# One chunk of a row's contraction moved ahead, a wider selection and a split product in the tail of an adaLN decode block

## The chip, the cores and the metric

The kernel runs on one core of a Trainium2 chip. The metric is the device time of one execution in microseconds, as the median over runs. All matmuls are fp32; the profile shows each fp32 matmul as two instructions (two passes) on TensorE, which is called PE in the profile (its weight loads: PEld). VectorE is DVE, ScalarE is ACT, GpSimd is POOL, SyncE is SP.

## What is computed

A decode step for four batch rows, one token each, D = 512, with a modulation from a conditioning vector c:

```python
mod = (silu(c) @ w_mod).reshape(4, 6, 1, -1)
sa, ca, ga, sb, cb, gb = (mod[:, i] for i in range(6))
h = layernorm(x) * (1 + ca) + sa
x = x + ga * attention(h, k_cache, v_cache, wq, wo)   # 32 query heads, 8 kv heads, 4096 positions, 128 wide
h = layernorm(x) * (1 + cb) + sb
u = gelu(einsum("bsd,sf->bdf", layernorm(h), w1) + b1)  # S = 1, F = 1792
y = einsum("bdf,fs->bds", u, w2) + b2
x = x + gb * transpose(y)
```

As there is one token per row, the mixer's first product is an outer product of the 512 channels with 1792 hidden units, followed by gelu and a weighted sum over the hidden units.

## The kernel before, in words

The 4 x 8 pairs of batch row and kv head are numbered 0 to 31. For each of them one 2 MB key tile and one 2 MB value tile come from memory on the SP queue. The steps for a pair are scores (line 216), the maximum over rows and columns (lines 224 to 247), the exponential on ACT (249), 32x32 transposes on DVE (253), the product with the values (275 to 293), a copy (301), a selection that folds the four column groups of the result into one vector per head (`pick`, 308), a scaling by the sum (321), the projection with wo (326) and the sum over heads (342).

Batch row b's mixer starts when its eight pairs are done. The hidden units are cut into 14 chunks of 128 (NF = 14). DVE expands a chunk (line 423), ACT applies the gelu, PE contracts the chunk with w2. For rows 0 to 2 a chunk's contraction is one matmul of 512 columns into one of four column groups of 32, chosen by the chunk's number (`contract_wide`, 433); the four groups are folded at the end (`gather_up`, 495). For the last row, row 3, each chunk is four matmuls of 128 columns, one for each column group (`contract`, 427), in `finish` (527).

Pairs 0 to 23 run in a loop. From pair 24 on, the order is written out by hand in the string PLAN (625 to 634): each word is one step, and the words' order is the order in which every engine's queue gets its instructions. Small letters and capitals are different steps; "s26" is the scores of pair 26, "a27" the selection of pair 27, "p31" the projection of pair 31. "x" expands two chunks of row 2, "g" applies the gelu to the oldest expanded pair of chunks, "c" contracts the oldest pair that has had its gelu. "f" scales one block of wo with the gate. The loads are the words with L. The engines run through their queues in order and wait for each other by semaphores.

The last line of PLAN is the tail, behind the last projection p31: "zs" takes the statistics of row 3 on DVE (line 363); "zq" starts the sums over all partitions with a small matmul that adds the epsilon (line 372); "zg" adds the statistics to it by a second matmul (line 377), which waits for zs; "c" twice contracts the chunks 10 to 13 of row 2, the chunks 12 and 13 lying in a spare piece of a load buffer, which the profile names kv; "zx" copies the row; "zm" normalises and modulates it into h (lines 394 to 404); "zq" and "zg" do the second statistics; "zb0" and "zb1" spread h over the partitions (line 411); "zw0" makes the first of the four parts (k = 0 to 3) of the last modulation product, the gate gb (`modmm`, 196); "zn" normalises; "zc" folds row 2's contraction (line 353). T2 and T3 make ACT load the tables of the square root and the gelu. Then `finish` runs row 3's 14 chunks in seven groups, makes the rest of the gate's product behind chunk 1 (line 540), and writes the output.

Selection. The result of the product with the values has four column groups; `pick` folds them with a matmul whose moving operand has four columns, one per query head. WIDE (line 24) repeats these columns for some pairs: for pair 27 (NS - 5) the four columns are repeated 24 times, so 96 columns move, and for pair 28 32 times, so 128 columns. Only the first four columns of the result are read:

```python
WIDE = {NS - 5: 24, NS - 4: 32}
...
n, m = po.shape[-1] // DH, WIDE.get(i, 1)
pt = ps_m.tile([P, m, REP], F32, name="pt", tag="m")
OT[i] = pt[:, 0]
```

Of the kernel before, what the change touches and what calls it, by code (L numbers as in the profile page):

```python
# [19 lines left out]
NS = B * HKV  # L20
NSM = 3 * NF + 16 + 1


WIDE = {NS - 5: 24, NS - 4: 32}
NARROW = NS - 3


# [1 line left out]
def adaln_decode(ctx: ExitStack, tc: tile.TileContext, small, x, wmod, wq, kk, kv, vv, wo, out):  # L29
# [166 lines left out]
    def modmm(pm, t, ks=range(4)):  # L196
        for k in ks:
            for c in range(4):
                mm(pm[32 * c:32 * c + 32, :], sT8[:, k].rearrange("p b r -> p (b r)"),
                   WM[t][:, k, c * P:(c + 1) * P], start=(k == 0), stop=(k == 3))  # L200
# [107 lines left out]
    def pick(i):  # L308
        po = PV.pop(i)
        n, m = po.shape[-1] // DH, WIDE.get(i, 1)  # L310
        if i in OT:
# [38 lines left out]
    def fold_groups(pool, acc, tag):  # L350
        pc = pool.tile([P, P], F32, name="pc", tag=tag)
        for c in range(4):
            mm(pc[32 * c:32 * c + 32, :], first, acc[:, c * P:(c + 1) * P], start=True, stop=True)
        return pc
# [68 lines left out]
    def expand(u, hb, wr, js):  # L423
        for e, j in enumerate(js):
            dv.tensor_scalar(u[:, e, :], hb, wr[:, j:j + 1], b1[:, j:j + 1], op0=OP.mult, op1=OP.add)  # L425

    def contract(py, u, js):
        for e, j in enumerate(js):
            for c in range(4):
                mm(py[32 * c:32 * c + 32, :], w2[:, j:j + 1].to_broadcast([P, 32]),  # L430
                   u[:, e, c * P:(c + 1) * P], start=(j == 0), stop=(j == NF - 1))

    def contract_wide(py, u, js):
        for e, j in enumerate(js):
            q = j % 4
            mm(py[32 * q:32 * q + 32, :], w2[:, j:j + 1].to_broadcast([P, 32]), u[:, e, :],  # L436
               start=(j < 4), stop=(j >= NF - 4))

    class Mixer:
# [48 lines left out]
        def consume(self, most=9):  # L488
# [3 lines left out]
                (contract_wide if self.wide else contract)(self.py, u, js)  # L492
            del self.done[:most]

        def gather_up(self):
            yw = wk.tile([P, D], F32, name="yw", tag="yw", bufs=1)
            dv.tensor_copy(yw, self.py)
            self.py = fold_groups(ps_e, yw, "e")
# [27 lines left out]

    def finish(b, pg, py, hb, wr):
        uu = ring.tile([P, 16, D], F32, name="uu", tag="kv")
        for js in ((0,), (1,), (2, 3, 4), (5, 6, 7), (8, 9, 10), (11, 12), (13,)):
            j = js[0]  # L530
            if j < 2:
                nc.scalar.activation(uu[:, j], hb, AF.Gelu_apprx_tanh, bias=b1[:, j:j + 1], scale=wr[:, j:j + 1])
                u = uu[:, j:j + 1]
            else:
                u = uu[:, j:j + len(js)]
                expand(u, hb, wr, js)
                nc.scalar.activation(u, u, AF.Gelu_apprx_tanh)  # L537
            contract(py, u, js)
            if j == 1:
                modmm(pg, 5, (1, 2, 3))  # L540
        mix.close()
        dv.tensor_mul(osb[:, :B - 1], ZK, pg.unsqueeze(1).to_broadcast([P, B - 1, P]))
        dv.tensor_add(osb[:, :B - 1], osb[:, :B - 1], XK[:, :B - 1])
        gbl = cst.tile([P, P], F32, name="gbl")
        dv.tensor_copy(gbl, pg)
        dst = out.rearrange("b (c n) -> b c n", c=4)
        for e in range(B - 1):
            (nc.scalar if e == B - 2 else nc.sync).dma_start(dst[e], osb[8 * e:P:32, e])
        dv.scalar_tensor_tensor(osb[:, b], py, b2, gbl, op0=OP.add, op1=OP.mult)
        dv.tensor_add(osb[:, b], osb[:, b], XK[:, b])  # L550
        nc.sync.dma_start(dst[b], osb[8 * b:P:32, b])
# [23 lines left out]
    mix = None  # L575
    for i in range(NS - HKV):
# [22 lines left out]
        if i and i % HKV == 0:  # L599
            mix = Mixer(i // HKV - 1)  # L600
# [14 lines left out]
        if i == NS - HKV - 2:  # L615
# [4 lines left out]
    mix, row = Mixer(B - 2), Mixer(B - 1)  # L620
# [9 lines left out]
    LV28 L28 a27 g X30 t29.1 t29.0 l29 L29 s31 A27 LV29 b30 p27 x B30 S31 c c m31 e30 P27 X31 v28.0 f LT LV30  # L630
    b31 v28.1 B31 f e31 LV31 l30 V28 L30 t30.1 l31 L31 a28 t31.1 A28 p28 v29.0 v29.1 t30.0 f P28 V29 v30.0 a29
    v30.1 A29 LW p29 f v30.2 v30.3 t31.0 P29 g V30 Y y a30 A30 p30 E x v31.0 f v31.1 v31.2 v31.3 V31 z31 a31 I A31 p31
    zs g zq zg T2 c zx c zm zq zb0 T3 zg zb1 zw0 zn zc
    """
    TABLE = {"s": scores, "S": row_max, "m": turn_max, "X": col_max, "b": spread_max, "B": copy_max, "e": expo,
             "l": sums, "L": scale, "V": copy_v, "a": pick, "A": copy_o, "P": add_up,
             "LP": load_pair}
    MIX = {"F": mix.fold, "R": mix.residual, "G": mix.gather, "M": mix.modulate, "H": mix.gather, "Q": mix.spread,
           "N": mix.normalise, "g": mix.gelu, "c": lambda: mix.consume(1), "zc": mix.gather_up, "zq": row.gather_eps,
           "zg": row.gather,  # L640
           "zm": row.modulate, "zn": row.normalise}
    for step in PLAN.split():
        op, k = step.rstrip("0123456789."), step.lstrip("abcdefghijklmnopqrstuvwxyzABCDEFGHIJKLMNOPQRSTUVWXYZ")
# [52 lines left out]
        elif op == "zb":  # L696
            if i == 0:
                py = ps_s.tile([P, 8, P], F32, name="py3", tag="s")
            row.spread(py[:, 4:], (2 * i, 2 * i + 1))
    finish(B - 1, pgx[:, 0], py[:, 0], row.hb, row.wr)  # L700


# [32 lines left out]
```

## Time and profile before

| | us |
|---|---|
| median of 3 runs | 387.23 (387.15 to 387.37) |
| the profiled execution's own time | 387.3 |
| its span, first to last instruction | 385.2 |
| PE busy | 295.1 (77% of the span) |
| DVE busy | 195.4 (51%) |
| ACT busy | 111.5 (29%) |
| memory read | 157.32 MB, 408 GB/s over the span |
| share of the last chain in transfers | 54% |
| mean granted PE clock | 0.892 |

All lines come from one execution, whose time line starts with the first instruction. A line of the time line has the start in us, the time that the merged group takes in us, engine, line of the kernel, operation, destination and sources, shapes and count; in brackets stands the idle time of the engine just before and what ended it. In the chain of waits, each piece of time is put down to the instruction which the end was waiting for just then. In a table by stretches, each engine's busy time is followed by the number of its instructions, and PEclk is the granted clock of TensorE as a share of full speed.

### The profile page before, as it was taken

The page shows a single profiled execution, that of the slowest core. Times are in us where ns is not written, and L with a number is a line of the kernel's source. Part 1 is how long each engine was busy: PE and PEld are TensorE (multiplying, and loading weights), DVE is VectorE, ACT ScalarE, POOL GpSimd, SP SyncE. Part 2 cuts the span into 40 slices and gives each one's busy share as a digit, 9 for nine tenths or more (in the row PEclk, how much of TensorE's full clock was granted, in tenths as well). Part 3 has the DMA queues.
Part 4 walks back from the last instruction along what each step waited for, and adds up shares of the span by engine and source line. Part 5 has one row for each costly group of instructions (what it writes and reads, how often), then busy time and mean ns, then how long its engine had stood idle before and what let it go on. Part 6 is the DMA issues. An engine that isn't in the chain of part 4 may idle for free.

```text
span 385.2 us, 5574 instructions
## 1 busy us (share of the span) xinstructions
PE 295.1 (77%) x2376; PEld 116.2 (30%) x2376; DVE 195.4 (51%) x386; ACT 111.5 (29%) x141; POOL 8.5 (2%) x30
## 2 busy tenths in 40 slices
PE   0865778865856939879877868799777897999984
PEld 0111122311223303334322322343222353344653
DVE  0120252620442614664766545648665566788756
ACT  1001111121110111112567211115674103758166
POOL 1200000000000000000000000000000000000000
PEclk9998555985995886998999998989999998999999
DMA  8999999999999999999999999999999999999920
GB/s 331 436 436 436 407 456 436 407 439 429 423 444 432 424 436 432 434 436 434 436 435 436 434 433 430 425 429 427 432 434 432 430 432 424 432 423 427 416 101 3
DMA packets 7408, 157.68 MB, mean 409 GB/s; under 512 B 964, under 2 KB 1236, under 8 KB 1496
## 3 DMA queue, kind: packets, MB, share of 16 engines
q1 hardware_dynamic: 7376, 157.33, 95.2%
q8 instruction: 18, 0.29, 0.3%
q14 instruction: 6, 0.05, 0.0%
q10 hardware_dynamic: 8, 0.00, 0.0%
HBM read 157.32 MB, written 0.01 MB: 408 GB/s over the span
## 4 chain that ended last, share of the span: by engine, by line
DMA 54%; PE 32%; DVE 8%; ACT 4%; issue 1%; POOL 1%; SPq 0%; ACTq 0%
DMA kv<-in_kv 42%; PE s L221 10%; PE pv L281 7%; DMA wm<-in_wmod 5%; DMA kv<-in_kk 4%; DVE m L226 3%; PE s L113 2%; DVE p L257 2%; DMA sm<-in_small 2%; PE pa L332 2%; PE pt L318 1%; PE pb L241 1%; ACT uu L537 1%; PE pm L205 1%; PE pve L293 1%; PE pm L230 1%
## 5 line engine op out<-in xcount | busy, mean ns | idle before, releaser
L221 PE MATMUL s<-kv,QT 128*32 128x512 f32 x512 | 79.0, 745 | 42.1 <-DMA kv<-in_kv 38.5
L226 DVE TENSOR_REDUCE m<-s 128x1 f32<-128x1024 f32 x32 | 39.2, 1224 | 101.9 <-PE s L221 101.7
L251 ACT ACTIVATE p<-s,nm 128x1024 f32<-128x1024 f32 x32 | 35.6, 1114 | 182.7 <-DVE nm L246 182.6
L281 PE MATMUL pv<-kv,p 128*32 128x512 f32 x464 | 67.1, 646 | 0.5 <-DMA kv<-in_kv 0.5
L221 PEld LDWEIGHTS s<-kv,QT 128*32 128x32 f32 x512 | 16.5, 126 | 88.5 <-DMA kv<-in_kv 54.8
L318 PEld LDWEIGHTS pt<-g,po 128*128 128x128 f32 x236 | 30.4, 200 | 28.5 <-issue 21.2
L332 PE MATMUL pa<-wo,oT 128*32 128x512 f32 x240 | 33.6, 633 | 4.6 <-DVE oT L324 4.5
L318 PE MATMUL pt<-g,po 128*128 128x4 f32 (+2 forms) x236 | 33.1, 264 | 1.5 <-DVE po L304 1.0
L257 DVE STREAM_TRANSPOSE p<-p 128x1024 f32<-128x1024 f32 x25 | 30.8, 1233 | 0.0
L304 DVE COPY po<-pv 128x512 f32<-128x512 f32 x29 | 20.0, 688 | 15.5 <-PE pv L281 15.5
L235 DVE TENSOR_REDUCE mx<-pm 1x128 f32<-1x512 f32 x32 | 21.3, 669 | 1.1 <-PE pm L230 1.1
L425 DVE TENSOR_SCALAR u<-hb,wr,sm 128x512 f32<-128x512 f32 x40 | 19.9, 539 | 1.9 <-POOL wr L420 1.0
L481 ACT ACTIVATE u<-u 128x1024 f32<-128x1024 f32 x20 | 20.4, 1051 | 1.5 <-DVE u L425 1.4
L251 ACT ACT_TABLE_LOAD x11 | 14.1, 1283 | 20.4 <-DVE nm L246 20.4
L348 DVE TENSOR_TENSOR acc<-acc,pa 128x512 f32<-128x512 f32 x26 | 17.8, 686 | 3.1 <-PE pa L332 3.1
L241 PEld LDWEIGHTS pb<-neg,mx 1*128 1x128 f32 x64 | 10.0, 194 | 26.9 <-DVE mx L235 25.2
L113 PE MATMUL s<-wm,sT 128*4 128x512 f32 x16 | 9.0, 725 | 11.3 <-DVE sT L99 11.3
L481 ACT ACT_TABLE_LOAD x13 | 16.7, 1283 | 0.2
L281 PEld LDWEIGHTS pv<-kv,p 128*32 128x32 f32 x464 | 13.3, 146 | 6.2 <-issue 2.3
L230 PE MATMUL pm<-ident,m 128*1 128x128 f32 x32 | 9.2, 286 | 7.6 <-DVE m L226 3.5
L241 PE MATMUL pb<-neg,mx 1*128 1x1 f32 x64 | 12.7, 265 | 2.1 <-DVE mx L235 2.1
L436 PE MATMUL py<-u,sm 128*32 128x512 f32 x80 | 13.5, 593 | 0.4 <-ACT u L481 0.4
(134 smaller groups left out, 207.9 us busy)
## 6 DMA issues: line engine op xcount, KB each, us to landing
kv<-in_kv SPq DMA_DIRECT2D x28, 4096.0 KB, 21.9
wq<-in_wq SPq DMA_DIRECT2D x2, 4096.0 KB, 16.2
wo<-in_wo SPq DMA_DIRECT2D x4, 2048.0 KB
kv<-in_kv SPq DMA_DIRECT2D x4, 2048.0 KB, 19.5
wm<-in_wmod SPq DMA_DIRECT2D x2, 2048.0 KB, 14.4
kv<-in_kk SPq DMA_DIRECT2D x1, 4096.0 KB
kv<-in_vv SPq DMA_DIRECT2D x3, 1024.0 KB
wm<-in_wmod SPq DMA_DIRECT2D x1, 1024.0 KB
```

The source lines that it names most:

```text
L221: mm(s[32 * c:32 * c + 32, n * 512:(n + 1) * 512], QT[:, b, h, :], KT[i][:, (n * 4 + c) * 512:(n * 4 + c + 1) * 512], start=True, stop=True)
L226: dv.tensor_reduce(M[i], S[i], axis=AX.X, op=OP.max)
L235: dv.tensor_reduce(mx, M[i].rearrange("o (c r) -> o r c", c=4).unsqueeze(1).to_broadcast([1, 4, 32, 4]), axis=AX.X, op=OP.max)
L241: mm(pb, M[i].rearrange("o c r -> o (c r)"), neg1, start=True, stop=True)
L251: nc.scalar.activation(p, S[i], AF.Exp, bias=M.pop(i), accum_out=l)
L257: dv.transpose(PL[i][0], PL[i][0])
L281: mm(PV[i][32 * q:32 * q + 32, :], pT[:, 128 * k:128 * k + 128:4], VT[i][:, 4 * k:4 * k + 4, :].rearrange("p j d -> p (j d)"), start=(k < ...
L304: dv.tensor_copy(PV[i], pv)
L318: mm(pt, po[:, c * DH:(c + 1) * DH], sel.unsqueeze(1).to_broadcast([P, m, REP]), start=(c == 0), stop=(c == n - 1))
L332: mm(pa[32 * g:32 * g + 32, :], oT[:, g:g + 1].to_broadcast([P, 32]), wo_t[h][:, g, :], start=True, stop=True)
L425: dv.tensor_scalar(u[:, e, :], hb, wr[:, j:j + 1], b1[:, j:j + 1], op0=OP.mult, op1=OP.add)
L481: nc.scalar.activation(u, u, AF.Gelu_apprx_tanh)
```

## The change

There are three edits.

1. Pair 27's selection moves 128 columns (32 repeats) instead of 96 (24 repeats).
2. A new step "k" (`consume_one`) contracts one chunk, the first of the oldest pair of chunks that has had its gelu, and leaves the other one in the list. It stands behind the first "zq" and ahead of "zg" in the tail's line of PLAN. The first of the two "c" steps then contracts one chunk in place of two.
3. In `finish`, part k = 1 of the last modulation product goes ahead of chunk 0; parts 2 and 3 stay behind chunk 1.

```diff
-WIDE = {NS - 5: 24, NS - 4: 32}
+WIDE = {NS - 5: 32, NS - 4: 32}
...
+        def consume_one(self):
+            u, js = self.done[0]
+            contract_wide(self.py, u, js[:1])
+            self.done[0] = (u[:, 1:], js[1:])
...
     def finish(b, pg, py, hb, wr):
         uu = ring.tile([P, 16, D], F32, name="uu", tag="kv")
+        modmm(pg, 5, (1,))
         for js in ((0,), (1,), (2, 3, 4), (5, 6, 7), (8, 9, 10), (11, 12), (13,)):
...
             if j == 1:
-                modmm(pg, 5, (1, 2, 3))
+                modmm(pg, 5, (2, 3))
...
-    zs g zq zg T2 c zx c zm zq zb0 T3 zg zb1 zw0 zn zc
+    zs g zq k zg T2 c zx c zm zq zb0 T3 zg zb1 zw0 zn zc
...
-           "N": mix.normalise, "g": mix.gelu, "c": lambda: mix.consume(1), "zc": mix.gather_up, "zq": row.gather_eps,
+           "N": mix.normalise, "g": mix.gelu, "c": lambda: mix.consume(1), "k": mix.consume_one, "zc": mix.gather_up, "zq": row.gather_eps,
```

## The prediction

> **What bounds the kernel now.** I read three views: the slices of the page (where the transfers end), the chain of waits from there on, and the TensorE (PE) instructions in order of time around each edit. In the page's 40 slices (9.6 us each, busy share in tenths) the transfers read:
>
> ```profile
> DMA  8999999999999999999999999999999999999920
> ```
>
> The reader is to see that the 16 DMA engines are at 8 or 9 to the end of slice 38, 366 us, at 2 in the next and at 0 in the last. Until about 367 us (the last wait for a load, quoted below, ends at 367.14) the transfers set the time; after it comes a tail of 18 us in which no load is awaited. No edit touches a load. So only what lies on the chain of the tail can count; here is its middle and its end.
>
> ```profile
> 370.40 0.40 PE pst L377 x2
> 370.81 0.99 PE py L436 x8
> 371.80 0.33 PE pst L372 x2
> 372.13 0.03 issue
> 372.16 0.68 PE py L411 x4
> ...
> 375.87 4.11 ACT uu L537 x3
> 379.99 0.01 issue
> 379.99 1.05 ACT uu L537
> 381.04 0.04 issue
> 381.09 0.99 PE py L430 x24
> ```
>
> The statistics of row 3 go DVE (stm), PE (pst, line 377), DVE again, and come back to PE as the spread of h (py, line 411). From there ScalarE's gelus run without a hole to 381.04, and the last contraction and the output follow. The last chain is serial: what is lost at line 377 is lost at the end. Around it PE does this:
>
> ```profile
> 369.70 0.40 PE L372 MATMUL pst<-epsr,ones 1*128 1x24 f32 x2
> 370.40 0.40 PE L377 MATMUL pst<-stm,ones 128*128 128x24 f32 x2 [0.31 <-DVE stm L367]
> 370.74 0.62 PE L436 MATMUL py<-u,sm 128*32 128x512 f32 x2
> 370.75 0.62 PE L436 MATMUL py<-kv,sm 128*32 128x512 f32 x2
> 371.19 0.60 PE L436 MATMUL py<-u,sm 128*32 128x512 f32 x2
> 371.20 0.60 PE L436 MATMUL py<-kv,sm 128*32 128x512 f32 x2
> 371.73 0.40 PE L372 MATMUL pst<-epsr,ones 1*128 1x24 f32 x2
> ...
> 373.48 0.42 PE L199 MATMUL pgx<-kv,sT 128*32 128x128 f32 x8
> ```
>
> Each fp32 matmul is two instructions (passes). The four chunks of the two steps "c" (10 and 11 from u, 12 and 13 from kv) go to four column groups: all four first passes start at 370.74 to 370.75, all four second ones at 371.19 to 371.20. They run side by side.
>
> **The change, part by part.** *The chunk moved forward (step k).* It issues one matmul, two passes of 512 columns, and two weight loads, on PE alone; no transfer, no other queue. Chunk 10 had its gelu long before (the pair's gelu is the step "g" behind P29), so k waits for nothing. It is put between line 372 at 369.70 and line 377 at 370.40, where PE stands idle for 0.31 us. What it takes there, from the rows: a pair of small matmuls followed by a 512-column pass is 370.74 - 370.40 = 0.34 apart, so k starts at 369.70 + 0.34 = 370.04. Its second pass uses the same column group and comes 371.19 - 370.74 = 0.45 later, 370.49. From a last 512-column pass to the next matmul over all columns is 371.73 - 371.20 = 0.53, so line 377 starts at 371.02 instead of 370.40: 0.62 us late. Queued behind k is just this matmul, and DVE waits for it (mean and variance), then h, then all of the tail.
>
> What k takes away later: the block at 370.74 has three chunks instead of four, and as they run side by side it is no shorter; gain 0. Could PE make good the delay before the spread at line 411? That needs h, which comes through DVE from line 377:
>
> ```profile
> 371.66 0.35 DVE L403 SCALAR_TENSOR_TENSOR h<-a,ye,prep 128x128 f32<-128x128 f32 x1
> ```
>
> h is done at 372.01, PE is done with line 372 at 372.13, and the spread starts at 372.16: the two paths meet within 0.12 us, and both hang on line 377. So the delay passes whole. Bounds: at the least, no drain at either border, a start 0.24 behind 369.70 (the closest distance between the pair at 348.26 and the scores at 348.50 below) and two passes of 0.45 end at 370.84, 0.44 late; at the most the whole block of 0.99 from the chain is set behind line 372's end at 370.10, 371.09, 0.69 late. I take 0.62, since its three distances are from neighbours of the same shapes.
>
> The Trainium skill, page "TensorEngine Tiling (Array Packing)", section "Key Properties", says that changing the tiling mode drains TensorE. The trace agrees as far as it goes: 0.53 from pass to full-width matmul against 0.45 from pass to pass. Without that rule the sum would be 0.44 late, with it 0.62; k adds one such change each way.
>
> *Head 27 in 32 columns instead of 24.* Four matmuls, eight passes, move 128 columns instead of 96; only the first four of the result are read. Head 28 already has that shape, so its price stands in the trace:
>
> ```profile
> 347.29 0.97 PEld L318 LDWEIGHTS pt<-g,po 128*128 128x128 f32 x8 [0.67 <-DVE rl L270]
> 347.29 1.13 PE L318 MATMUL pt<-g,po 128*128 128x96 f32 x8 [0.46 <-DVE rl L270]
> 348.26 0.31 PE L265 MATMUL pl<-g,l 128*128 128x4 f32 x2
> 348.50 1.93 PE L221 MATMUL s<-kv,QT 128*32 128x512 f32 x16
> ...
> 356.06 0.97 PEld L318 LDWEIGHTS pt<-g,po 128*128 128x128 f32 x8
> 356.06 1.16 PE L318 MATMUL pt<-g,po 128*128 128x128 f32 x8
> ...
> 367.14 0.14 PEld L293 LDWEIGHTS pve<-kv,p 128*32 128x32 f32 x4 [0.18 <-DMA kv<-in_vv]
> ```
>
> Weight loads pace both, 0.97 us; the wider one takes 1.16 instead of 1.13, so 0.03 us, and 8 x 32 columns at 0.45/512 us, 0.23, if the columns came on top. PE then waits for the last values anyway, 0.18 us in its weight queue at 367.14, behind which the tail begins. That wait covers 0.03 wholly and 0.23 but for 0.05. I take 0; the cover gone, 0.03 to 0.23.
>
> *Part of the last modulation product moved forward.* Four matmuls, eight passes of 128 columns, leave the twelve behind chunk 1 of row 3 and go ahead of chunk 0, behind line 353. PE alone, no waits of their own, as the weights of step zw have been in use since 373.48.
>
> ```profile
> 375.22 0.42 PE L430 MATMUL py<-uu,sm 128*32 128x128 f32 x8 [0.79 <-ACT uu L532]
> ...
> 376.17 0.84 PE L199 MATMUL pgx<-kv,sT 128*32 128x128 f32 x24
> 377.39 0.86 PE L430 MATMUL py<-uu,sm 128*32 128x128 f32 x24 [0.39 <-ACT uu L537]
> ...
> 380.29 0.55 DVE L542 TENSOR_TENSOR osb<-zk,pgx 128x384 f32<-128x384 f32 x1
> ```
>
> Eight such passes take 0.42 (line 199 at 373.48), and the hole before chunk 0 is 0.79, ended by ScalarE: hidden, 0. Were the hole gone it would cost 0.42. The 0.3 it saves at 376.17 falls into the 0.39 that PE waits for ScalarE anyway, and the product is not read before 380.29: 0.
>
> **Sum.** 0.62 + 0 + 0 = 0.62 us on the profiled execution's 387.3 us (span 385.2, 2.1 around it). That execution is 0.07 above the median, so on the median 387.23 + 0.62 = 387.85 us, 0.16% slower. About 0.2%, 0.77 us, is what a measurement of this kernel can tell from no change; the forecast stays inside it, by little.
>
> **The rivals.** *The clock goes cold in the tail.* Windows of 3.41 us, in the phase in which the clock changed in this trace (columns window, length, PE busy, clock, DMA share, GB/s):
>
> ```profile
> 315.70:319.12 3.42, 2.90 (x28) 0.99 1.05 446
> 319.12:322.53 3.41, 3.41 (x20) 0.50 0.93 404
> ...
> 373.73:377.14 3.41, 2.10 (x56) 1.00 0.01 2
> 377.14:380.56 3.42, 2.15 (x64) 1.00 0.02 5
> 380.56:383.97 3.41, 1.39 (x41) 1.00 0.01 2
> ```
>
> A window busy for 2.90 was followed by a clock of 0.50, so the tail's windows with 2.10 and 2.15 cannot be called safe, and a tail 0.62 later puts fewer of the last contractions into the second of them. What cold costs: eight passes of 512 columns took 1.86 at the clock of 0.50 and 1.10 at 1.00.
>
> ```profile
> 318.89 1.86 PE L281 MATMUL pv<-kv,p 128*32 128x512 f32 x8 [0.52 <-DMA kv<-in_kv]
> ...
> 354.06 1.10 PE L281 MATMUL pv<-kv,p 128*32 128x512 f32 x8
> ...
> 381.08 0.68 PEld L430 LDWEIGHTS py<-uu,sm 128*32 128x32 f32 x24 [0.35 <-ACT uu L537]
> ```
>
> That is 0.76 for 4096 columns, 0.57 for a group of 24 passes of 128. Two groups lie in the last window; of 1.14 the 0.35 that PE waits before the second is covered, so 0.8 us: 387.85 + 0.8 = 388.65. Against it: PE gets more work early on, and before stayed at 1.00. The Trainium skill, page "TensorE: Matmul & The Clock Gate", Part 1, describes a free-running window of 3413 ns after which an idle array falls to half its clock; the windows above agree, and by it the phase may differ from run to run. Chance 0.22.
>
> *More of it comes through*: the 0.23 of the wider selection is not covered, which decides once the wait at 367.14 is gone. 387.85 + 0.05 to 0.23 is 387.9 to 388.1, 388.05 as a mark. For it: that wait is only 0.18. Against: the row of head 28, where the columns hide under the weight loads. Chance 0.12.
>
> *k is free* (the other side): PE takes k's passes in beside line 377, or line 377 is let past, and with a chunk less the block at 370.74 frees PE sooner. The place is the 0.31 idle at 370.40; it decides once k takes under 0.31 there. Then nothing is late, and at best the 0.12 by which PE trails h at 372.13 is won: 387.1 to 387.25, 387.2. Against it stands that every row shows PE in order. Chance 0.08.
>
> *Ordinary executions are cold in the tail and the change warms them*: two passes in the block at 370.74 would take 0.8 longer there, the last window another 0.8; with both warm, less 0.62, that is 387.23 - 1.0 = 386.25. Against it: the profiled execution had a clock of 1.00 to the end and was no faster than the median. Chance 0.10.
>
> **How the numbers follow.** The forecast has 0.48: 387.65 to 388.05 as its own range, of which 0.40 within 388.00 and 0.08 above. Slower by over 0.2%: 0.08 + 0.22 + 0.12 = 0.42. Within: 0.40 + 0.08 = 0.48. Faster: 0.10. The range 387.1 to 388.7 holds the forecast, the free k, the wider selection, and the nearer half of the cold clock; it leaves out about 0.10 below and 0.10 above. It takes in the bounds 0.44 and 0.69.
>
> **What would show it.** In the profile of the changed kernel, two passes of line 436 stand alone near 370.0 of this timeline, line 377 starts 1.3 behind line 372 instead of 0.70, the block of chunks 11 to 13 lasts 1.0 as before, and everything from there to the end is 0.6 later. The selection of head 27 takes 1.16. Eight passes of line 199 stand before chunk 0 and ScalarE's gelus have no new hole. Wrong it would be if line 377 starts within 0.9 of line 372, if the clock shows 0.50 before 382, or if the wait for the last values at 367.14 is gone.

## The result

The changed kernel takes 387.91 us (median of 19 executions) against 387.23 us before (19 executions): 0.68 us more. The ratio is 1.0017, with a 95% interval from 1.001 to 1.0024. The forecast was 387.85.

The chain of waits of the changed kernel, from the last projection on (start in us, length, what):

```profile
369.80 0.33 PE pst L372 x2
370.13 0.97 PE py L436 x2
371.10 0.33 PE pst L377 x2
371.43 0.99 PE py L436 x6
372.42 0.33 PE pst L372 x2
372.75 0.04 issue
372.79 0.68 PE py L411 x4
...
380.63 1.05 ACT uu L543
381.68 0.04 issue
381.72 0.99 PE py L430 x24
```

A new piece of 0.97 us, the single chunk, stands between lines 372 and 377, and the block behind line 377 is as long as before with six passes in it instead of eight (0.99). The last contraction starts at 381.72, before at 381.09.

The matmuls on PE in order of time in the same execution (start, time, line, operation, count, idle time before):

```profile
368.72 1.08 PE L337 MATMUL pgx<-wo,oT 128*32 128x128 f32 x32
369.73 0.40 PE L372 MATMUL pst<-epsr,ones 1*128 1x24 f32 x2
370.06 1.04 PE L436 MATMUL py<-u,sm 128*32 128x512 f32 x2
371.03 0.40 PE L377 MATMUL pst<-stm,ones 128*128 128x24 f32 x2
...
374.86 0.43 PE L199 MATMUL pgx<-kv,sT 128*32 128x128 f32 x8
375.86 0.42 PE L430 MATMUL py<-uu,sm 128*32 128x128 f32 x8 [0.57 <-ACT uu L538]
```

Line 377 follows line 372 by 371.03 - 369.73 = 1.30 us; it was 0.70. The idle time before line 377, which statistics on DVE had ended, is gone; its place is taken by PE's own queue. DVE shows the other side of it, a wait of 0.89 us for line 377 where it was 0.29 (in the DVE instructions in order of time, the mean and variance of row 3, first before, then in the changed kernel):

```profile
370.84 0.27 DVE L382 BATCH_NORM_AGGREGATE mv<-pst 128x2 f32<-128x24 f32 x1 [0.29 <-PE pst L377]
```

```profile
371.47 0.27 DVE L382 BATCH_NORM_AGGREGATE mv<-pst 128x2 f32<-128x24 f32 x1 [0.89 <-PE pst L377]
```

The part of the modulation product that was moved, at 374.86, ends before ScalarE releases chunk 0 at 375.86; 0.57 us of the hole are left.

### The profile page after: what moved, and what is told of

The parts are those of the page before. It is cut to its first block, busy times and chain, and to the rows that moved or that the text cites. A ratio compares the mean times of both kernels' runs of the same rounds, so it can differ in the third digit from the quotient of the medians.

```text
span 385.8 us, 5574 instructions
## 1 busy us (share of the span) xinstructions
PE 296.9 (77%) x2376; PEld 118.4 (31%) x2376; DVE 195.8 (51%) x386; ACT 111.5 (29%) x141; POOL 8.5 (2%) x30
## 4 chain that ended last, share of the span: by engine, by line
DMA 59%; PE 31%; DVE 6%; ACT 2%; issue 1%; POOL 1%; SPq 0%; ACTq 0%; DVEq 0%
DMA kv<-in_kv 57%; PE s L221 8%; PE pv L281 7%; PE s L113 3%; DVE m L226 2%; PE pa L332 2%; PE qs L128 2%; DMA sm<-in_small 2%; PE pt L318 2%; DVE p L257 2%; ACT uu L543 1%; PE pb L241 1%; PE pve L293 1%; PE py L436 1%; PE pm L230 1%
## 5 line engine op out<-in xcount | busy, mean ns | idle before, releaser
L221 PE MATMUL s<-kv,QT 128*32 128x512 f32 x512 | 76.0, 713 | 45.3 <-DMA kv<-in_kv 42.6
L281 PE MATMUL pv<-kv,p 128*32 128x512 f32 x464 | 70.2, 673 | 0.9 <-DMA kv<-in_kv 0.9
L318 PEld LDWEIGHTS pt<-g,po 128*128 128x128 f32 x236 | 31.3, 206 | 28.3 <-issue 21.0
L332 PE MATMUL pa<-wo,oT 128*32 128x512 f32 x240 | 34.5, 648 | 4.4 <-DVE oT L324 4.2
L318 PE MATMUL pt<-g,po 128*128 128x4 f32 (+1 forms) x236 | 34.1, 268 | 1.5 <-DVE po L304 1.0
L113 PE MATMUL s<-wm,sT 128*4 128x512 f32 x16 | 9.8, 779 | 11.2 <-DVE sT L99 11.2
L436 PE MATMUL py<-u,sm 128*32 128x512 f32 x80 | 14.5, 593 | 0.0
```

The costliest lines, as they stand in the source:

```text
L113: mm(s0[0:B, t * D:(t + 1) * D], sT[:, k, :], wm01[:, t, k, :], start=(k == 0), stop=(k == 3))
L221: mm(s[32 * c:32 * c + 32, n * 512:(n + 1) * 512], QT[:, b, h, :], KT[i][:, (n * 4 + c) * 512:(n * 4 + c + 1) * 512], start=True, stop=True)
L281: mm(PV[i][32 * q:32 * q + 32, :], pT[:, 128 * k:128 * k + 128:4], VT[i][:, 4 * k:4 * k + 4, :].rearrange("p j d -> p (j d)"), start=(k < ...
L318: mm(pt, po[:, c * DH:(c + 1) * DH], sel.unsqueeze(1).to_broadcast([P, m, REP]), start=(c == 0), stop=(c == n - 1))
L332: mm(pa[32 * g:32 * g + 32, :], oT[:, g:g + 1].to_broadcast([P, 32]), wo_t[h][:, g, :], start=True, stop=True)
```

## The experiments

In all of them "before" ran on the same chip; the medians of before in the three batches were 387.32, 387.33 and 387.27 us.

### One edit at a time

First, only the chunk moved forward, with the other two edits undone:

```diff
-WIDE = {NS - 5: 32, NS - 4: 32}
+WIDE = {NS - 5: 24, NS - 4: 32}
...
-        modmm(pg, 5, (1,))
...
-                modmm(pg, 5, (2, 3))
+                modmm(pg, 5, (1, 2, 3))
```

> Only the chunk moved forward; the selection stays at 24 repeats and the product in one piece behind chunk 1. My theory (k delays line 377 by 0.62 us and that is the whole change): 0.6 us above before (0.5 to 0.7), line 377 starts 1.3 us behind line 372. Rival (the wider selection or the product carries part of it): 0.3 us or less above before.

Measured: 387.93 us, 0.61 above before. The ratio is 1.0032 (1.0009 to 1.0055); it lies above the ratio of the medians, 1.0016, because two executions, at 389.68 and 392.59, are in it. Line 377 follows line 372 by 1.30 us.

```profile
370.09 0.40 PE L372 MATMUL pst<-epsr,ones 1*128 1x24 f32 x2
370.42 1.04 PE L436 MATMUL py<-u,sm 128*32 128x512 f32 x2
371.39 0.40 PE L377 MATMUL pst<-stm,ones 128*128 128x24 f32 x2
```

Second, the other two edits without the chunk:

```diff
-    zs g zq k zg T2 c zx c zm zq zb0 T3 zg zb1 zw0 zn zc
+    zs g zq zg T2 c zx c zm zq zb0 T3 zg zb1 zw0 zn zc
```

> The wider selection and the split product, without the chunk moved forward. My theory: no difference from before, within 0.15 us; line 377 again 0.70 us behind line 372. Rival (the other two edits carry part): 0.3 to 0.7 us above before.

Measured: 387.37 us, 0.05 above before; ratio 1.0 (0.9991 to 1.0009). In its PE instructions line 377 is back at 370.46 - 369.75 = 0.71 behind line 372, and waits for DVE again:

```profile
369.75 0.40 PE L372 MATMUL pst<-epsr,ones 1*128 1x24 f32 x2
370.46 0.40 PE L377 MATMUL pst<-stm,ones 128*128 128x24 f32 x2 [0.31 <-DVE stm L367]
```

What follows: the whole of the change's 0.6 us is the chunk. The rival, by which the other edits carry a part, falls.

### What the chunk's price goes by

Two chunks in k's place instead of one:

```diff
-    zs g zq k zg T2 c zx c zm zq zb0 T3 zg zb1 zw0 zn zc
+    zs g zq c zg T2 zx c zm zq zb0 T3 zg zb1 zw0 zn zc
```

> The changed kernel, but chunks 10 and 11 both contracted at the place of k. My theory (chunks in different column groups run side by side): the same 0.6 us above before as with one chunk, at most 0.05 more, and the block of 12 and 13 that is left lasts 1.0 us as before. Rival (the price goes by chunks): a second pair of passes, 0.9 us more, 1.5 us above before.

Measured: 387.93 us, 0.61 above before, the same as with one chunk; ratio 1.0015 (1.0006 to 1.0024). The PE instructions:

```profile
369.65 0.40 PE L372 MATMUL pst<-epsr,ones 1*128 1x24 f32 x2
369.97 1.05 PE L436 MATMUL py<-u,sm 128*32 128x512 f32 x4
370.96 0.40 PE L377 MATMUL pst<-stm,ones 128*128 128x24 f32 x2
371.29 1.05 PE L436 MATMUL py<-kv,sm 128*32 128x512 f32 x4
```

Four passes take 1.05 us where two took 1.04, and line 377 is 1.31 behind line 372. A price by chunks would have put it at 2.2. The chunks of different column groups do run side by side: the first one at the new place takes the time of a whole block, a second one beside it next to nothing, and the block that they leave gets no shorter.

Half a chunk in k's place: columns 0 to 255 ahead of line 377, the other half with the block behind it (the new step "r", `consume_rest`; the rest of the edit only sets COLS to 256 and names the step).

```diff
         def consume_one(self):
             u, js = self.done[0]
-            contract_wide(self.py, u, js[:1])
-            self.done[0] = (u[:, 1:], js[1:])
+            q = js[0] % 4
+            w = w2[:, js[0]:js[0] + 1].to_broadcast([P, 32])
+            mm(self.py[32 * q:32 * q + 32, 0:COLS], w, u[:, 0, 0:COLS], start=False, stop=False)
+
+        def consume_rest(self):
+            ...
+            mm(self.py[32 * q:32 * q + 32, COLS:D], w, u[:, 0, COLS:D], start=False, stop=True)
+            self.done[0] = (u[:, 1:], js[1:])
+            self.consume(1)
...
-    zs g zq k zg T2 c zx c zm zq zb0 T3 zg zb1 zw0 zn zc
+    zs g zq k zg T2 r zx c zm zq zb0 T3 zg zb1 zw0 zn zc
```

> The changed kernel, but k contracts only columns 0 to 255 of chunk 10, and the other 256 are contracted with the block behind line 377. My theory (the price is the streaming beyond the hole of 0.31 us): passes of 0.225 instead of 0.45, so line 377 comes 0.18 us later than before, and the end 0.2 us (0.1 to 0.3). Rival (a fixed price of switching between full-width and 32-column matmuls): 0.4 to 0.6 us above before.

Measured: 387.39 us, 0.07 above before; ratio 1.0002 (0.9993 to 1.0011), which doesn't tell it from before. The trace is sharper than the time:

```profile
369.69 0.40 PE L373 MATMUL pst<-epsr,ones 1*128 1x24 f32 x2
370.01 0.62 PE L500 MATMUL py<-u,sm 128*32 128x256 f32 x2
370.56 0.40 PE L378 MATMUL pst<-stm,ones 128*128 128x24 f32 x2
```

The distance is 0.87 us, 0.17 more than before, where 0.18 was worked out. Half the columns cost little more than a quarter of the price, because PE's wait before line 377 covers the first 0.37 us: before, line 377 follows line 372 by 0.70, and by 0.33 where it waits for nothing (the next trace). With this the trace excludes a fixed price of switching of 0.4 to 0.6 us; the interval of the time alone would not.

### Which side of line 372

The chunk directly behind the projection, with line 372 behind it:

```diff
-    zs g zq k zg T2 c zx c zm zq zb0 T3 zg zb1 zw0 zn zc
+    zs g k zq zg T2 c zx c zm zq zb0 T3 zg zb1 zw0 zn zc
```

> The changed kernel with k ahead of the epsilon matmul (line 372) instead of behind it, so directly behind the projection, which also uses 32-column groups. My theory (a switch to full-width matmuls and back costs its own time): k starts 0.1 us behind the last projection pass, line 372 comes 1.0 us behind k's start, line 377 0.22 us behind line 372; line 377 then comes 0.35 us later than before (0.3 to 0.45) and so does the end. Rival (the switch costs nothing, only streaming counts): 0.6 us above before as with k behind line 372.

Measured: 387.77 us, 0.44 above before; ratio 1.0016 (0.9986 to 1.0046), too wide to tell it from either theory, as one execution took 392.8. The trace:

```profile
368.82 1.08 PE L337 MATMUL pgx<-wo,oT 128*32 128x128 f32 x32
369.73 1.02 PE L436 MATMUL py<-u,sm 128*32 128x512 f32 x2
370.68 0.40 PE L372 MATMUL pst<-epsr,ones 1*128 1x24 f32 x2
371.01 0.40 PE L377 MATMUL pst<-stm,ones 128*128 128x24 f32 x2
```

From the start of the projection to line 377 it is 371.01 - 368.82 = 2.19 us, against 2.31 in the changed kernel and 370.40 - 368.69 = 1.71 before (368.69 is the projection's start there). In the changed kernel it is 371.03 - 368.72. So the order saves 0.12 us of the 0.60, not the 0.27 that I had expected (0.62 - 0.35): line 372 came 0.95 behind the chunk (1.0 worked out), but line 377 came 0.33 behind line 372, not 0.22. Between the projection and line 377 the matmuls here change once between 32 columns and full width, at line 372, as they do in the kernel before; in the changed kernel they change three times. So the 0.12 is what two such changes cost together. The half chunk agrees: without a chunk line 377 follows line 372 by 0.33, with half a chunk by 0.87, with a whole one by 1.30. If the price beyond the changes goes evenly by columns, 0.43 for each half, 0.87 - 0.33 - 0.43 = 0.11 us is left for the two changes, an estimate.

### Is the block behind line 377 on the path?

The kernel before, without chunks 10 to 13 of row 2. These four are left out of the sum, so the result for row 2 lacks them. Besides the line shown, the flag that closes the sum moves to the last chunks that are left, here and in the two kernels of the next section.

```diff
-    zs g zq zg T2 c zx c zm zq zb0 T3 zg zb1 zw0 zn zc
+    zs g zq zg T2 zx zm zq zb0 T3 zg zb1 zw0 zn zc
```

> The kernel before without the contraction of chunks 10 to 13 of row 2 (left out of the output; nothing of the change). My theory (the spread of h waits for DVE, with PE ready at most 0.12 us later): 0 to 0.12 us below before. Rival (the 0.99 us of this block in the chain of waits are on the path, so that moving part of it away could have paid): 0.5 to 0.9 us below before.

Measured: 388.04 us, 0.71 above before, with executions from 386.97 to 388.53; ratio 1.0015 (1.0007 to 1.0024). With a block of matmuls less, the kernel is slower; both expectations missed. Its PE instructions and its table by stretches (window, length, busy time of PE, PEld, DVE, ACT, POOL with counts, granted clock, DMA share, GB/s) say why:

```profile
370.51 0.40 PE L377 MATMUL pst<-stm,ones 128*128 128x24 f32 x2 [0.31 <-DVE stm L367]
370.84 0.40 PE L372 MATMUL pst<-epsr,ones 1*128 1x24 f32 x2
372.26 1.19 PE L411 MATMUL py<-h,ident 128*128 128x128 f32 x4 [1.03 <-DVE h L403]
...
373.54 1.20 PE L411 MATMUL py<-h,ident 128*128 128x128 f32 x4
```

```profile
369.00:372.00 3.00, 1.92 (x38) 1.48 (x30) 1.59 (x7) 0.47 (x2) 0.00 (x0) 0.98 0.06 22
372.00:375.00 3.00, 2.74 (x18) 2.53 (x22) 1.41 (x5) 1.44 (x3) 0.76 (x2) 0.50 0.00 0
375.00:378.00 3.00, 2.29 (x44) 1.30 (x40) 2.44 (x6) 2.92 (x4) 0.00 (x0) 0.50 0.01 3
378.00:382.00 4.00, 4.00 (x80) 3.51 (x76) 3.90 (x9) 4.00 (x4) 0.00 (x0) 0.50 0.01 4
```

Two things happen. The spread at line 411 starts 372.26 - 370.51 = 1.75 us behind line 377, against 1.76 before, and PE stands idle for 1.03 us until h comes from DVE: leaving the block out gains 0.01 us here, although the chain of waits put 0.99 us down to it. And PE is busy for only 1.92 of the 3 us from 369 (2.69 before), and the granted clock falls to 0.50 from 372 to 382. The spreads take 1.19 and 1.20 instead of 0.68 and 0.69, and there the time is lost: in the chains of waits, from the start of the first spread to ScalarE's step behind the second one (hb, line 419) it is 374.77 - 372.26 = 2.51 us, before 373.58 - 372.16 = 1.42. At the end PE, not ScalarE, sets the time (two pieces of its chain of waits):

```profile
377.77 1.28 PE pgx L199 x24
379.05 4.24 PE py L430 x96
```

But this costs next to nothing: from the start of hb to the end of the last step on DVE it is 9.22 us, before 9.20. Of the 11 executions 8 took 387.73 us or more, while 34 of the 35 of before took 387.6 or less, so the block that is left out is the cause of the slower median. The executions near 387 are what a warm clock would give; that the others were cold is shown for the profiled one alone, which took 388.29.

### What keeps the clock up

Two of the four chunks left in, so that PE works as long as before in half of the column groups (chunks 12 and 13 are left out of the sum):

```diff
-    zs g zq zg T2 c zx c zm zq zb0 T3 zg zb1 zw0 zn zc
+    zs g zq zg T2 c zx zm zq zb0 T3 zg zb1 zw0 zn zc
```

> The kernel before with only chunks 10 and 11 contracted behind line 377; 12 and 13 are left out of the output. PE is busy as long as before, with two of four column groups. First reading (the clock goes by the time in which PE works): the clock stays at 1.00 to the end as in before, and the time is within 0.1 us of it. Second reading (the clock goes by how much of the array works): the clock shows 0.50 behind 372 in part of the executions, as where the whole block was left out, and the median lies 0.3 to 0.8 us above before. The end without a cold clock is the same in both, as the block is not on the path.

Measured: 387.32 us, 0.05 above before; ratio 1.0002 (0.9993 to 1.0011). Over the whole tail the clock is 1.00:

```profile
372.00:382.00 10.00, 7.28 (x164) 4.90 (x163) 8.49 (x21) 9.03 (x10) 0.76 (x2) 1.00 0.01 2
```

And the changed kernel with k alone, without chunks 11 to 13 (left out of the sum):

```diff
-    zs g zq k zg T2 c zx c zm zq zb0 T3 zg zb1 zw0 zn zc
+    zs g zq k zg T2 zx zm zq zb0 T3 zg zb1 zw0 zn zc
```

> The changed kernel with k, but without chunks 11 to 13 behind line 377; these three are left out of the output. My theory on the path: line 377 comes 0.62 us late, as in the changed kernel. On the clock, first reading (time in which PE works): k puts back the 0.9 us that the left-out block had, the clock stays at 1.00, 0.6 us above before. Second reading (share of the array): one chunk in one column group is not enough, the clock shows 0.50 behind 372 in part of the executions, and the median lies 1.0 to 1.8 us above before.

Measured: 387.95 us, 0.68 above before; ratio 1.0018 (1.0006 to 1.003). Line 377 follows line 372 by 1.31 us, as in the changed kernel. The clock did not stay up in the profiled execution:

```profile
373.00:374.00 1.00, 1.00 (x9) 1.00 (x10) 0.47 (x4) 0.86 (x2) 0.00 (x0) 1.00 0.00 0
374.00:375.00 1.00, 1.00 (x18) 0.58 (x20) 0.62 (x2) 0.64 (x1) 0.70 (x2) 0.58 0.00 0
375.00:376.00 1.00, 0.85 (x17) 0.40 (x9) 0.86 (x2) 0.92 (x3) 0.06 (x1) 0.50 0.00 0
376.00:377.00 1.00, 0.95 (x16) 0.48 (x20) 1.00 (x4) 1.00 (x2) 0.00 (x0) 0.50 0.03 8
377.00:378.00 1.00, 0.96 (x24) 0.64 (x16) 1.00 (x4) 1.00 (x1) 0.00 (x0) 0.72 0.08 16
```

It was 0.50 for one window, from 374.15 to 377.56. The spreads were all but done by then (374.34), and the window cost next to nothing, under the time in which ScalarE's gelus set the pace: from the start of the first spread to the end of the last step on DVE it is 383.56 - 372.91 = 10.65 us, in the changed kernel 383.41 - 372.79 = 10.62. Two of the ten executions took 388.78 and 388.93, some 0.9 above the median; whether the clock fell at the spreads in them is not shown. The first run fits the reading by working time, the second neither reading wholly: k's 0.97 us kept the median at the price of line 377's delay, but not the clock at 1.00. Nor does busy time as the profile shows it decide alone: in the 3.41 us just ahead of the fall PE was busy for 2.38 us here and for 2.45 in the run without the block, while windows of 2.10 and 2.15 in the kernel before were followed by 1.00. Whether the clock goes by working time or by the share of the array is not settled.

### The two edits without a price

A selection far wider than the change's, 256 columns for pair 27 in the kernel before:

```diff
-WIDE = {NS - 5: 24, NS - 4: 32}
+WIDE = {NS - 5: 64, NS - 4: 32}
```

> The kernel before with 64 repeats in pair 27's selection, so 256 columns: eight passes of 0.225 us take 1.8 instead of 1.13, 0.7 to 0.8 us more on PE at 347 us. My theory (the waits for the last values cover what PE loses before them, of which the last is 0.18 us): 0 to 0.6 us above before, and the wait for the values at 367 is gone. Rival (the waits for transfers between 355 and 367 cover all of it): within 0.15 us of before, with the wait at 367 as long as before.

Measured: 387.64 us, 0.31 above before; ratio 1.0012 (1.0004 to 1.0021). PE loses 0.87 us at the place (from the selection to line 265: 349.35 - 347.51 = 1.84, before 348.26 - 347.29 = 0.97):

```profile
347.51 2.00 PE L318 MATMUL pt<-g,po 128*128 128x256 f32 x8 [0.46 <-DVE rl L270]
349.35 0.28 PE L265 MATMUL pl<-g,l 128*128 128x4 f32 x2
...
368.23 0.61 PE L299 MATMUL pt<-p,kv 128*128 128x4 f32 x4
```

The first matmul of the tail, line 299, comes 20.72 us behind the selection; before it was 367.63 - 347.29 = 20.34. So 0.38 of 0.87 came through and 0.49 was covered. The wait for the values at 367 is gone, as expected; it stood in the last group of line 293's matmuls, which starts 366.38 - 347.51 = 18.87 us behind the selection, before 365.49 - 347.29 = 18.20, so 0.67 late. From there to line 299 another 0.29 is covered, and 0.20 ahead of it, where the weight queue's wait for values at 362 fell from 0.85 us to 0.30. In the changed kernel the selection itself is as the row of pair 28 said, and the wait for the last values is still there:

```profile
347.34 1.16 PE L318 MATMUL pt<-g,po 128*128 128x128 f32 x8 [0.46 <-DVE rl L270]
...
367.18 0.14 PEld L293 LDWEIGHTS pve<-kv,p 128*32 128x32 f32 x4 [0.18 <-DMA kv<-in_vv]
```

All three parts of the modulation product ahead of chunk 0, in the kernel before:

```diff
         uu = ring.tile([P, 16, D], F32, name="uu", tag="kv")
+        modmm(pg, 5, (1, 2, 3))
...
             if j == 1:
-                modmm(pg, 5, (1, 2, 3))
+                pass
```

> The kernel before with all three parts of the modulation product ahead of chunk 0, 24 passes of 0.84 us in a hole of 0.79 us. My theory: within 0.15 us of before, the hole before chunk 0 nearly gone. Rival (it delays chunk 0 and what follows): 0.2 to 0.5 us above before.

Measured: 387.29 us, 0.04 below before; ratio 1.0 (0.9992 to 1.0009).

```profile
374.00 0.43 PE L353 MATMUL pc<-yw,g 128*32 128x128 f32 x8
374.22 0.86 PE L199 MATMUL pgx<-kv,sT 128*32 128x128 f32 x24
375.21 0.43 PE L430 MATMUL py<-uu,sm 128*32 128x128 f32 x8
```

Even three times the change's part fits into the hole: chunk 0 starts at 375.21, before at 375.22.

No kernel was faster than before beyond its interval, and the runs point to no version that would be: moving the block, or leaving it out, gains nothing on the path.

## Why the prediction was right

**The chunk moved forward.** The three distances held each for itself. k starts 370.06 - 369.73 = 0.33 behind line 372 (0.34 forecast). Its second pass starts at 370.51, 0.45 later (0.45), and line 377 another 371.03 - 370.51 = 0.52 later (0.53). Line 377 is late by 0.60 against 0.62. The upper bound of 0.69 and the lower one of 0.44 hold it between them. The median moved by 0.68; the 0.08 above the trace's 0.60 is within what the interval leaves open. One thing beside the sum was off: I put at 0.2% what a measurement can tell from no change, and 19 executions of each kernel told 0.17% from it, with an interval that begins at 0.1%.

**No gain from the shorter block.** Right, and for the two reasons given: two chunks in k's place cost what one does, and with the whole block gone the spread still comes 1.75 us behind line 377. The 0.12 us that I allowed a free k at best, for PE trailing h, were not there: with PE idle ahead of it the spread came 0.01 us sooner.

**The wider selection at 0.** Right in the sum. The 0.03 us by the row of pair 28 is what the changed kernel shows (1.16 against 1.13). The cover was mis-sized: I put it at 0.18, the one wait at 367.14, and then 0.05 of 0.23 would come through; the run with 256 columns shows 0.49 of 0.87 covered, 0.29 of it at that wait and 0.20 ahead of it. So the rival "more of it comes through" had less for it than the 0.12 that I gave it.

**The product moved forward at 0.** Right: 0.57 us of the hole are left in the changed kernel, and three times as much still hid.

**The switch between matmul shapes.** Its share was somewhat too large. I set 0.44 without it and 0.62 with it, thus 0.18 for the two changes of shape that k adds, together with their spacing, and expected 0.27 to be saved by the order that has neither. The runs showed 0.12 for the two: line 377 is 0.60 late in the changed kernel and 2.19 - 1.71 = 0.48 late with k ahead of line 372. The Trainium skill, page "TensorEngine Tiling (Array Packing)", section "Key Properties", says that a change of the tiling mode drains the array. The trace agrees as far as these 0.12 us go; the streaming of 2 x 512 columns is the larger part, as half a chunk shows.

**The cold clock.** It did not come in the changed kernel's profile: 1.00 in all windows until the end. What it can cost is shown in the run without the block: clock 0.50 from 372 to 382, span 386.4 against 385.2, 1.2 us, of which 2.51 - 1.42 = 1.09 lie at the spreads. My 0.8 us was for the last window alone, a place that no run had cold to its end, so that price stays open; the spreads, where the price was paid, were not in my sum for this rival. The Trainium skill, page "TensorE: Matmul & The Clock Gate", Part 1, has the clock halve after an idle window and the windows run free of the kernel. On the first the measurement differs: PE was busy for 2.45 of the 3.41 us ahead of the fall behind 372. My prediction set that rule beside its own rows and said that they agree; they do so in the length of the window only, as PE was busy for 2.90 of 3.42 us ahead of the fall at 319.12. The length agrees in the run without the block too: 0.50 from 371.88 to 382.12 is three times 3.41 us. Executions of one kernel from 386.97 to 388.53 fit windows that run free of it, without showing it.

## What to carry to other kernels

A hole on an in-order engine is as wide as the wait that ends it: work put there is free up to that width (0.31 us of idle time here) and lengthens the path by what it takes beyond it (0.17 us for half a chunk, 0.60 for a whole one), and matmuls that run side by side give nothing back when one of them is taken from their group. A piece that the chain of waits lists beside another path of the same length can be worth nothing; leaving it out for one run tells. Before matmuls are taken from a thin tail, look at the granted clock: what is off the path may still be what keeps it at 1.00.

## What the runs showed of the hardware

- Taking 1 us of matmuls out of an 18 us tail made the kernel slower by 0.71 us in the median: the granted clock fell to 0.50 for 10 us in the profiled execution.
- Two chunks in two column groups kept the clock at 1.00 as well as four in four (387.32 against 387.27 us).
- Where a cold window falls decides its price: from 372 to 382 it took 1.2 us of span, 1.09 of it at the two spreads; from 374.15 to 377.56 (k alone), behind the spreads, 0.03 us.
- Two changes between 32-column and full-width matmuls cost 0.12 us together (2.31 against 2.19 us from the projection to line 377).
